# Moving the conversion of one expert's second weight matrix from one product to the next

## The chip, the cores and the metric

The kernel runs on one core of one Trainium2 chip. The metric is the device time of one execution in microseconds (us). The engines are TensorE (PE in the profile; its weight loads are PEld), VectorE (DVE), ScalarE (ACT), GpSimd (POOL) and SyncE (SP), whose queue issues most of the DMAs.

## The reference

A random-feature attention is followed by a gated product and a routed layer of experts, all in float32:

```python
q_p, k_p = phi(q_s), phi(k_s)            # exp(h - max h), h = x omega^T - |x|^2/2
num / den                                # from kv = k_p^T v and z = sum k_p; x is [1152, 512]
h = ((x @ w1) * (x @ w2)) @ w3           # 512 -> 1024 -> 1024
x = h @ w_out                            # [1152, 512]
logits = x @ w_gate                      # 8 experts; argmax picks one for each token
h = np.maximum(disp[e] @ w1[e], 0)       # [capacity, 1024], capacity 288
out[i] = gate_w[i] * (h @ w2[e])[pos[i]] # tokens over the capacity stay zero
```

Here `disp[e]` holds the tokens sent to expert e, in order, as far as the capacity goes.

## The kernel before

Every float32 product is made of three TensorE products: each operand is split into a high part (a cast that ACT makes) and a low part (the difference, a subtraction on DVE or POOL), and high x high, low x high and high x low are summed in PSUM (the list `PASS`). `w3 @ w_out` is multiplied out beforehand into eight tiles `W`, so that the tokens' gated values go straight to 512 features.

The experts run in chunks of 288 token slots, called runs. Two runs are written out, r0 and r1; a loop at the end takes whatever chunks are left over, and has none here. A run consists of these generators, each of which gives way after a piece of its products:

- `to_features` (letter t for r0, T for r1): transposes the gathered rows and splits them into `xc`.
- `product` (p, P): multiplies `W` with `xc` into four PSUM banks `x2p`, one for each 128 of the 512 features, 24 matmuls each. Two steps take the first two slices of all four banks; then a step each finishes bank 0, 1, 2 and 3 with 18 matmuls and splits it: ACT casts it to `x2h` (L843), DVE subtracts to `x2l` (L844).
- `hidden` (h, H): the first weights of the expert, in four quarters q of two 128-wide half steps f. The first quarter's two half steps go side by side over the four feature slices k, in 24 matmuls; each of the other six half steps takes 12. After a half step ACT casts it with the Relu (L865) and DVE makes the low part (L866) into `hh`. The PSUM banks come from the pools `pm` (two banks, even f) and `pa` (four banks, odd f).
- `result_t` (s, S): the second weights of the expert times `hh`. For r1 a first group of 24 matmuls (L899, PSUM `r_yt`) makes 128 of the 512 output features transposed, then 72 matmuls (L913) and six transposes the rest; DVE scales by the gate (`r_yo`, L874), and POOL scatters three groups of 96 rows with an indirect DMA each (L875).

The expert's weights come from HBM by numbers known only at run time, in four quarters for the first matrix (`e1`) and four for the second (`e2`). `e_task` makes a task of each quarter: its load, issued on SP (L743) by `pump` as soon as one of two slots in its ring (`wr` for even quarters, `u` for odd ones) is free, and three stages:

```python
push(key, ring, load, [("A", lambda t: hi(t, 0), False),   # ACT: cast of the first half, 128x512
                       ("AV", both, False),                # DVE: its low part; ACT: second cast
                       ("P", lambda t: lo(t, 1), True)])   # POOL: second low part; frees the slot
```

`tick` advances the tasks by one stage each, at most one for an engine and at most two tasks at a time; so four quarters take nine ticks. A task of an expert's weights is started only when its key is in the set `leave`:

```python
while todo and (todo[0]["key"][0][0] != "e" or todo[0]["key"][:2] in leave) and (...):
    active.append(todo.pop(0))
```

The string `END` writes the order out by hand: a generator's letter is one step of it, a dot is a tick, `x` asks for the e1 quarters of r1 and `y` for its e2 quarters, and the digits 1 to 4 give leave to e1 of r0, e2 of r0, e1 of r1 and e2 of r1. When `S` is first reached, `got2` ticks until all e2 quarters of r1 are done. The instructions of every engine run in the order in which they are written (`in_order`, `keep_order`), so a cast that is written ahead of an eviction on ACT also runs ahead of it.

In the trace the digits of a run and of a matrix are left out of the names: `r_e_20h` is quarter 2, first half, high part, of e1 or of e2 of either run. In the order written here, the e1 quarters of r1 come before its e2 quarters.

Of the kernel before, what the change touches and what calls it, by code (L numbers as in the profile page):

```python
# [54 lines left out]

END = "l<kAkrArfAAArfw>AAAA>AA<At.ttLttMt>1K.p..K.p..Rp..p..p..RpF.2h..h.R.h..Fh..h..h..xh..h..s.TT.3sTT..sTT..s..ssy4P..P..P..P..P..P..P.H.H.H.H.H.HHHSSSS"


@with_exitstack
def attention_moe_kernel(ctx: ExitStack, tc: tile.TileContext, qT, kT, v, om, w1, w2, w3, wo, wg, e1, e2, cap, out):
# [901 lines left out]

    for p in END:
        if p == "A":
# [119 lines left out]
```

## Time and profile before

| | |
|---|---|
| median of three runs | 343.3 us (343.2 to 344.44) |
| profiled execution | 342.88 us, of which the span is 341.1 us |
| PE busy in the span | 326.2 us (96%) |
| DVE, ACT, POOL busy | 214.9, 146.4, 134.6 us (63%, 43%, 39%) |
| mean granted TensorE clock | 0.988 of full speed |

All times in the trace are counted from the start of the span. A row of the timeline gives start, duration, engine, line, operation, output <- inputs and, in brackets, how long the engine was idle before it and what ended that. Matmuls are pipelined, so that one is shown with some 0.29 us while the next starts 0.13 us after it; the starts are what tells the pace.

### The profile page before, as it was taken

Reading aid. Unit: us, or ns where it says so; the run is one execution under the profiler, and the core shown is the slowest. Engines: PE = TensorE matmul, PEld = TensorE weight load, DVE = VectorE, ACT = ScalarE, POOL = GpSimd, SP = SyncE. Lnnn points to the kernel's source line nnn. Section 1 sums busy time; section 2 is a strip of 40 time slices with the busy share of each in tenths; the row PEclk is TensorE's granted clock in tenths of the full one; section 3 lists DMA queues with packets and bytes.
Section 4 is the critical chain, followed back from the end, with each engine's and each line's share of the span. In section 5 each row is a group of like instructions: output and inputs, shape, how many; then the busy total and the mean of one; then the engine's idle time right before and its main releaser. Section 6 shows DMA issues by size and latency. Waiting matters only on the chain. (4 is left out here: it accounts for less than half of the span.)

```text
span 341.1 us, 7107 instructions
## 1 busy us (share of the span) xinstructions
PE 326.2 (96%) x2771; PEld 302.1 (89%) x2771; DVE 214.9 (63%) x426; ACT 146.4 (43%) x347; POOL 134.6 (39%) x118
## 2 busy tenths in 40 slices
PE   8899989999999999999999999999999999979991
PEld 6799879999998899898879988899799998969991
DVE  3979999999987854925695780562787435322110
ACT  4899899733221423424335422222635346232100
POOL 2737920233353224355547572015253612370011
PEclk9999999999999999999999999999999999998997
DMA  7985200243455729982435412966699933230001
GB/s 248 397 311 179 85 12 2 78 160 122 141 174 187 256 39 203 186 160 62 144 113 178 132 53 103 267 50 196 220 219 139 260 126 125 58 136 2 1 25 51
DMA packets 25147, 47.76 MB, mean 140 GB/s; under 512 B 3116, under 2 KB 12460, under 8 KB 25110
## 3 DMA queue, kind: packets, MB, share of 16 engines
q1 hardware_dynamic: 16950, 40.18, 39.1%
q10 hardware_dynamic: 7104, 3.54, 7.1%
q0 software_dynamic: 1056, 3.54, 3.7%
q8 instruction: 24, 0.39, 0.5%
q14 instruction: 13, 0.11, 0.1%
HBM read 38.98 MB, written 8.27 MB: 139 GB/s over the span
## 5 line engine op out<-in xcount | busy, mean ns | idle before, releaser
L433 PE MATMUL ab<-xh,w_hl 128*128 128x288 f32 x512 | 107.8, 299 | 1.0 <-ACT a_sb L437 0.8
L433 PEld LDWEIGHTS ab<-xh,w_hl 128*128 128x128 f32 x512 | 83.5, 188 | 3.6 <-issue 1.9
L433 PE MATMUL ab<-xl,w_hl 128*128 128x288 f32 x256 | 75.6, 295 | 0.0
L433 PEld LDWEIGHTS ab<-xl,w_hl 128*128 128x128 f32 x256 | 48.1, 188 | 0.0
L472 PE MATMUL W<-wo_hl,w_hl 128*128 128x512 f32 x192 | 46.4, 397 | 0.0
L472 PEld LDWEIGHTS W<-wo_hl,w_hl 128*128 128x128 f32 x192 | 35.5, 188 | 8.1 <-issue 0.5
L364 POOL TENSOR_TENSOR w_hl<-w_f,w_hl 128x512 fp32r<-128x512 f32 x22 | 29.7, 1364 | 7.7 <-ACT w_hl L360 6.3
L405 DVE STREAM_TRANSPOSE gs<-g 128x576 f32<-128x576 f32 x16 | 19.6, 1225 | 16.1 <-POOL g L446 16.0
L350 DVE TENSOR_SCALAR w_f<-w_raw 128x512 uint32<-128x512 uint32 x22 | 16.5, 749 | 17.7 <-POOL w_hl L364 16.9
L840 PE MATMUL r_x2p<-r_xc,W 128*128 128x288 f32 x192 | 26.8, 297 | 0.2 <-DVE r_yo L874 0.2
L840 PEld LDWEIGHTS r_x2p<-r_xc,W 128*128 128x128 f32 x192 | 25.8, 188 | 0.5 <-DVE r_yo L874 0.4
L360 ACT CAST w_hl<-w_f 128x512 fp32r<-128x512 f32 x22 | 13.7, 624 | 26.8 <-DVE w_f L355 26.5
L331 POOL TENSOR_TENSOR wo_hl<-wo_f,wo_hl 128x512 fp32r<-128x512 f32 x8 | 11.4, 1429 | 34.2 <-PE xT L276 18.4
L480 POOL TENSOR_TENSOR W<-W_raw,W 128x512 fp32r<-128x512 f32 x8 | 10.9, 1358 | 34.8 <-ACT u_all L503 23.6
L437 ACT COPY a_sb<-ab 128x288 f32<-128x288 f32 x32 | 12.7, 398 | 24.6 <-PE ab L433 24.0
L331 POOL TENSOR_TENSOR w_hl<-w_f,w_hl 128x512 fp32r<-128x512 f32 x10 | 14.0, 1403 | 22.4 <-ACT w_hl L330 22.4
L355 DVE SCALAR_TENSOR_TENSOR w_f<-w_raw,w_f 128x512 uint32<-128x512 uint32 x22 | 20.0, 909 | 0.6
L875 POOL DMA_INDIRECT out<-r_yo,r_odx x6 | 5.6, 932 | 35.6 <-DVE r_yo L874 22.7
L446 POOL TENSOR_TENSOR g<-a_sb,b_sb 128x288 f32<-128x288 f32 x12 | 11.6, 966 | 19.9 <-ACT b_sb L445 19.9
L448 DVE TENSOR_TENSOR g<-a_sb,ab 128x288 f32<-128x288 f32 x20 | 8.9, 446 | 14.1 <-PE ab L433 14.1
L210 PE MATMUL pjk<-om_hl,k_hl 128*128 128x256 f32 x108 | 15.1, 292 | 1.5 <-ACT k_hl L198 1.4
L210 PE MATMUL pjq<-om_hl,q_hl 128*128 128x256 f32 x108 | 16.3, 293 | 0.0
(233 smaller groups left out, 692.4 us busy)
## 6 DMA issues: line engine op xcount, KB each, us to landing
w_raw<-in_w SPq DMA_DIRECT2D x32, 512.0 KB, 3.6
wo_raw<-in_wo SPq DMA_DIRECT2D x8, 512.0 KB, 3.7
gd<-gs ACTq DMA_DIRECT2D x12, 288.0 KB, 6.0
v<-in_v SPq DMA_DIRECT2D x9, 260.0 KB, 5.4
k<-in_kT SPq DMA_DIRECT2D x9, 256.0 KB, 4.7
q<-in_qT SPq DMA_DIRECT2D x9, 256.0 KB, 7.2
out<-zero SPq DMA_DIRECT2D x1, 2304.0 KB, 7.9
r_e_0r<-in_e SPq DMA_DIRECT2D x4, 512.0 KB, 4.9
```

Source lines behind the costliest of these rows:

```text
L210: nc.tensor.matmul(out=ps[:, r * 256:(r + 1) * 256], lhsT=t[:, s, k * 128:(k + 1) * 128], rhs=om_hl[:, w], start=(n == 0), stop=(n == 2))
L331: nc.gpsimd.tensor_tensor(out=hl[1], in0=f.bitcast(F32), in1=hl[0].bitcast(F32), op=ALU.subtract)
L350: V.tensor_scalar(out=f, in0=r[:, :, 1], scalar1=3, scalar2=0x3FFFFFF8, op0=ALU.logical_shift_left, op1=ALU.bitwise_and)
L355: V.scalar_tensor_tensor(out=t["f"], in0=r[:, :, 0], scalar=29, in1=t["f"], op0=ALU.logical_shift_right, op1=ALU.bitwise_or)
L360: A.copy(out=h[:, 0], in_=t["f"].bitcast(F32))
L364: nc.gpsimd.tensor_tensor(out=h[1], in0=t["f"].bitcast(F32), in1=h[0].bitcast(F32), op=ALU.subtract)
L405: V.transpose(out=sts[b][:, :, :, f % GF], in_=g_t[f][:, b * S:(b + 1) * S].rearrange("p (j t) -> p j t", t=32))
L433: nc.tensor.matmul(out=p[:, :C], lhsT=w12[f][w][s][:, k, :], rhs=xhl[c][r][:, k], start=(n == 0), stop=(n == 11))
L437: A.copy(out=abp[f, c], in_=p[:, :C])
L446: nc.gpsimd.tensor_tensor(out=g_t[f][:, c * C:(c + 1) * C], in0=abp.pop((f, c)), in1=b_sb, op=ALU.mult)
L472: nc.tensor.matmul(out=p, lhsT=w3_t[f, k // 4][s][:, k % 4, :], rhs=wo_t[k][r], start=(n == 0), stop=(n == 23))
L840: nc.tensor.matmul(out=p4[d][:, :C], lhsT=w_t[f][:, s, d * 128:(d + 1) * 128], rhs=xc[r][f // 4][:, f % 4], start=(f == 0 and (s, r) == (0 ...
```

## The change

The digit 4 moves from behind `y` to behind the last step of r1's `product`, and each of the first five steps of r1's `hidden` is followed by two ticks in place of one. Nothing is added or taken out; the order of casts and subtractions against the evictions changes.

```diff
-END = "l<kAkrArfAAArfw>AAAA>AA<At.ttLttMt>1K.p..K.p..Rp..p..p..RpF.2h..h.R.h..Fh..h..h..xh..h..s.TT.3sTT..sTT..s..ssy4P..P..P..P..P..P..P.H.H.H.H.H.HHHSSSS"
+END = "l<kAkrArfAAArfw>AAAA>AA<At.ttLttMt>1K.p..K.p..Rp..p..p..RpF.2h..h.R.h..Fh..h..h..xh..h..s.TT.3sTT..sTT..s..ssyP..P..P..P..P..P..P4.H..H..H..H..H..HHHSSSS"
```

## Rows read from the trace of the kernel before

**Rows 1.** Table by stretches: start:end, length, busy time of each engine, PEclk, DMA share, GB/s.

```profile
256.00:270.30 14.30, 14.30 (x121) 14.29 (x120) 10.04 (x36) 7.65 (x17) 5.90 (x6) 1.00 0.88 186
...
300.43:317.82 17.39, 15.30 (x99) 14.31 (x97) 5.63 (x11) 5.75 (x13) 4.80 (x4) 0.90 0.15 57
```

**Rows 2.** Timeline of PE at r1's first expert product and the start of its last.

```profile
300.43 0.30 PE L861 MATMUL r_hp<-r_x2h,r_e_00h 128*128 128x288 f32 x1
...
301.89 0.29 PE L861 MATMUL r_hp<-r_x2h,r_e_00l 128*128 128x288 f32 x1
303.98 0.40 PE L861 MATMUL r_hp<-r_x2h,r_e_00h 128*128 128x288 f32 x1 [1.80 <-ACT r_x2h L843]
...
317.82 0.43 PE L899 MATMUL r_yt<-r_h,r_e_00h 128*128 128x288 f32 x2
```

**Rows 3.** Timeline of ACT over r1's product and first expert product.

```profile
293.42 0.40 ACT L843 CAST r_x2h<-r_x2p 128x288 fp32r<-128x288 f32 x1 [3.54 <-PE r_x2p L840]
...
295.82 0.40 ACT L843 CAST r_x2h<-r_x2p 128x288 fp32r<-128x288 f32 x1 [0.96 <-PE r_x2p L840]
302.50 0.62 ACT L756 CAST r_e_20h<-r_e_2r 128x512 fp32r<-128x512 f32 x1 [6.27 <-SPq L1007]
...
303.54 0.39 ACT L843 CAST r_x2h<-r_x2p 128x288 fp32r<-128x288 f32 x1
...
305.15 0.39 ACT L843 CAST r_x2h<-r_x2p 128x288 fp32r<-128x288 f32 x1
...
318.02 0.41 ACT L865 ACTIVATE r_h<-r_hp 128x288 fp32r<-128x288 f32 x1 [1.19 <-PE r_hp L861]
```

**Rows 4.** Timeline of SP: the load of e2's third quarter.

```profile
298.93 0.33 SPq L743 DMA_DIRECT2D r_e_2r<-in_e  x1
```

**Rows 5.** Timeline of POOL: r0's last scatter, then e1's third quarter.

```profile
296.66 0.92 POOL L875 DMA_INDIRECT out<-r_yo,r_odx  x1 [2.60 <-ACT r_x2h L843]
297.60 1.31 POOL L760 TENSOR_TENSOR r_e_20l<-r_e_2r,r_e_20h 128x512 fp32r<-128x512 f32 x1
```

**Rows 6.** Table by stretches: one stretch inside r1's first expert product.

```profile
306.10:309.20 3.10, 3.10 (x13) 3.10 (x14) 0.92 (x2) 0.82 (x2) 0.62 (x1) 0.51 0.00 0
```

**Rows 7.** Timeline of ACT over the first expert product of r0.

```profile
261.15 0.41 ACT L865 ACTIVATE r_h<-r_hp 128x288 fp32r<-128x288 f32 x1 [0.16 <-PE r_hp L861]
261.46 1.13 ACT L756 CAST r_e_10h<-r_e_1r 128x512 fp32r<-128x512 f32 x2
262.75 0.41 ACT L865 ACTIVATE r_h<-r_hp 128x288 fp32r<-128x288 f32 x1 [0.16 <-PE r_hp L861]
...
265.22 0.41 ACT L865 ACTIVATE r_h<-r_hp 128x288 fp32r<-128x288 f32 x1 [1.04 <-PE r_hp L861]
...
270.02 0.41 ACT L865 ACTIVATE r_h<-r_hp 128x288 fp32r<-128x288 f32 x1 [1.19 <-PE r_hp L861]
```

**Rows 8.** Timeline of PE: the first matmul of r0's first expert product.

```profile
256.17 0.30 PE L861 MATMUL r_hp<-r_x2h,r_e_00h 128*128 128x288 f32 x1
```

**Rows 9.** Timeline of POOL: two low halves of weights.

```profile
251.92 1.86 POOL L760 TENSOR_TENSOR r_e_30l<-r_e_3r,r_e_30h 128x512 fp32r<-128x512 f32 x1 [1.88 <-ACT r_e_30h L756]
...
262.67 1.28 POOL L760 TENSOR_TENSOR r_e_10l<-r_e_1r,r_e_10h 128x512 fp32r<-128x512 f32 x1 [0.30 <-ACT r_e_10h L756]
```

**Rows 10.** Timeline of DVE: two low halves of weights and two small additions.

```profile
247.11 1.79 DVE L760 TENSOR_TENSOR r_e_20l<-r_e_2r,r_e_20h 128x512 fp32r<-128x512 f32 x1
...
260.51 0.69 DVE L760 TENSOR_TENSOR r_e_00l<-r_e_0r,r_e_00h 128x512 fp32r<-128x512 f32 x1
...
263.06 0.90 DVE L944 TENSOR_TENSOR ni<-tm 96x1 int32<-96x1 f32 x1
...
264.03 0.15 DVE L947 TENSOR_TENSOR d<-ends 96x8 f32<-96x8 f32 x1
```

**Rows 11.** Timeline of POOL: r1's first and last scatter.

```profile
326.54 0.92 POOL L875 DMA_INDIRECT out<-r_yo,r_odx  x1 [19.81 <-DVE r_yo L874]
...
335.39 0.92 POOL L875 DMA_INDIRECT out<-r_yo,r_odx  x1 [2.58 <-DVEq L1007]
```

## Prediction, made before the changed kernel was run

> **What bounds the kernel now.** PE is busy for 326.2 of the 341.1 us, so the first view is the table by stretches: where is PE not busy, or not at full clock? For the expert products the two runs can be set side by side. In r0's first expert product PE is busy in all of 14.30 us at a granted clock of 1.00; in r1's it is busy in 15.30 of 17.39 us at 0.90 [rows 1]. Both do the same 96 matmuls. The second view, the timeline of PE, shows where the time goes in r1: twelve matmuls run at 0.13 us each from 300.43 to 301.89, the thirteenth starts at 303.98, and an ACT cast of `x2h` at L843 released it [rows 2]. The third view, the timeline of ACT, tells why that cast was late [rows 3]. Banks 0 and 1 of `x2p` were cast at 293.42 and 295.82, 2.40 us apart, which is the pace of their 18 matmuls; bank 2 was therefore full at 298.22 and bank 3 at 300.62. But bank 2 was cast at 303.54 and bank 3 at 305.15. The ACT row ahead of them is a cast of weights, at 302.50, for which ACT stood idle 6.27 us.
>
> That cast is of the third quarter of e2, and its data came late: SP issued the load at 298.93 [rows 4], because the slot came free only with POOL's low half of e1's third quarter at 297.60, which stood in POOL's queue behind r0's last scatter at 296.66 [rows 5]. So the chain is scatter, POOL subtraction, slot, load (3.57 us from 298.93 to 302.50), ACT cast, and behind that cast, by order alone, two evictions that have nothing to do with it. PE then pays twice: it waits, and in the stretch from 306.10 to 309.20 that follows the wait its granted clock is 0.51, the lower of its two levels, 1.2 GHz [rows 6].
>
> **The change part by part.** No instruction is added. What moves is the conversion of e2's four quarters for r1: eight casts on ACT, four subtractions on DVE, four on POOL.
>
> Which ticks go where: six ticks lie between digit 3 and `y`, and nine are needed for e1's four quarters, so the first three ticks among the P steps still go to e1, before and after. The other ten there belong to e2 before, and do nothing after. The new places hold eleven ticks (one behind digit 4, two behind each of five steps), and e2 needs nine: the last stage falls behind the fourth step, half step f = 4. Nothing is left over for `got2` to force.
>
> The loads don't move: a slot comes free with the POOL stage of e1's quarters, which is one of the same three ticks, so SP still issues e2's third quarter at about 298.93, with nothing queued differently. It lands at 302.5 as before, where no one waits for it until the cast behind half step f = 3, some 6 us later.
>
> What goes: without the weights' casts ahead of them, the casts of banks 2 and 3 start as PE ends them, at about 298.2 and 300.6. The cast takes 0.40 us [rows 3]; if the low part took 0.69 us, the length of a low half of weights nearly twice its size [rows 10], bank 3 would be complete at 301.7. The first expert product reaches slice 2 at 300.43 + 12 x 0.133 = 302.0 and slice 3 at 302.8. So both are there in time, with 1.1 us to spare, and PE should run through. What is late next: e1's third and fourth quarter, whose low halves end on POOL at 298.9 and, one such subtraction later, at 300.2; they are wanted after 48 and 72 matmuls, at 306.8 and 310.0. Nothing there.
>
> The size, by r0's product: from its first matmul at 256.17 [rows 8] to its last Relu cast at 270.02 it takes 13.85 us. One gap between its Relu casts is 2.47 us (262.75 to 265.22) instead of the 1.60 of the others [rows 7], since products of r1's routing lie between; without them it is 13.85 - 0.87 = 12.98 us. Put at r1's first matmul, 300.43, the last Relu cast comes at 313.41 instead of 318.02 [rows 3]: **4.61 us less**. By parts: 303.98 - 302.02 = 1.96 us is the first wait, 3.10 x (1 - 0.51) = 1.52 us the lower clock, and the remaining 1.13 us the second wait, for bank 3, between 303.98 and 306.10.
>
> What it costs: the eight casts now stand between the Relu casts. In r0's product that same pattern is in the trace, and that is why I take this cost as nothing: Relu cast, two weight casts (1.13 us), next Relu cast 1.60 us after the first, and the idle time of 0.16 us before it is ended by PE, so ACT still waits for PE and not PE for ACT [rows 7]. ACT would be full to 1.44 of 1.60 us for four half steps. If that cover went (casts only some 10% longer), evictions would lag, and PE would notice only when a bank is wanted again: f = 4 reuses the bank of f = 0, 3.3 us later. The low halves on DVE (0.69 us) [rows 10] and POOL (1.28 us) [rows 9] go once per half step, 1.97 us if one waits for the other, against a pace of 1.60: at worst they slip by 0.4 us per quarter. The second quarter-stage of e2 can start once f = 0 and f = 1 are done, at 303.6; four times 1.97 us later is 311.5. The first result product starts at 317.82 - 4.6 = 313.2 [rows 2] and wants the last half quarter after 21 matmuls, at 316.0. That is 4.5 us of slack. From below: could the moved work gain something where it was? In the P steps PE had no wait but the one counted; so no gain beyond the 4.61. From above, the slowest rows of such halves are 1.79 us on DVE [rows 10] and 1.86 us on POOL [rows 9]; what they would do is the second rival. I take the nearest rows, those of r0's product, which are the same work at the same place.
>
> One observation weighs against this. In r0's product a DVE addition of 96x1 elements took 0.90 us from 263.06, while one of 96x8 took 0.15 [rows 10]; the long one ended at 263.96, and a POOL subtraction of weights ran from 262.67 to 263.95 [rows 9]. The Trainium skill ("SBUF — State Buffer", section "Who interferes with whom") has a rule for it: a DVE instruction with both inputs in SBUF and a POOL instruction that reads SBUF take the same port, and whoever is second waits for the whole of the first. The trace agrees. By the rule each low half on DVE can wait for the POOL half of the quarter before, and the Relu's low part behind it as well; by the free durations alone it would not. The sum is the same by both, but the rule is a reason to give the second rival a chance at all.
>
> What follows the product moves as a block: the first scatter is released by DVE's scaled rows at 326.54, the last comes 8.85 us later, at 335.39 [rows 11], and all three hang on PE's result products.
>
> **The sum.** The profiled execution is 342.88 us (span 341.1 and 1.8 around it); less 4.6 that is 338.3. The median of the runs, 343.3, is 0.4 above it; less 4.6 that is 338.7. I forecast **338.5 us**, 1.4% faster. What a measurement of this kernel can tell from no change is about 0.5%, so from 341.6 to 345.0 counts as the same.
>
> **The rivals.**
> *The lower clock comes anyway* (in the changed kernel too, TensorE is at 1.2 GHz for some 3 us of this product). For it: that the drop is caused by the wait is read from their order only. Against it: r0's product, without a wait, is at 1.00 throughout [rows 1]. It gives back 1.5 us: 340.0. Chance 0.07.
>
> *The conversions become the chain* (DVE and POOL taking turns, then the casts too). They have from 303.6 to 316.0, which is 3.1 us per quarter. At the slowest rows, 1.79 + 1.86 = 3.65, they end at 318.2, 2.2 late: 340.7. If both casts (1.13) come in series as well, 4.78 per quarter, they end at 322.7, 6.7 late, and the wait in `result_t` brings the lower clock for another 1.5: 346.7, **slower than before**. The point from which it loses is 4.25 us per quarter (4.6 us late). For it: those rows exist. Against it: the halves in r0's product, 0.69 and 1.28, are far from it. Chances 0.06 for the partial loss, 0.04 for slower.
>
> *No change*: the gain is eaten at the end, because the scatters, each waiting for the one before, and not the products set it. For it: the last scatter is not released by its own data. Against it: the first one is, after 19.81 us idle [rows 11], so the series would start earlier. Or the casts stay where they were, if I have miscounted the ticks. 343. Chance 0.06.
>
> **How the numbers follow.** The forecast has 0.77, and its own spread is about 0.9 us either way, from the spread of the runs and from the two ways of counting. The range 337.6 to 340.8 takes in the rival with the clock and the partial loss and leaves out no change and slower. Faster by over 0.5%: 0.77 + 0.07 + 0.06 = 0.90; same 0.06; slower 0.04.
>
> **What would show it.** Right: in the changed profile the `x2h` casts of banks 2 and 3 start at about 298.2 and 300.6; PE has no wait in the first expert product; the granted clock there is 1.00; the first result product starts at about 313.2; the weight casts lie between Relu casts, until about 310; the span is some 336.5 us. Wrong: a PE wait at L861 that is still released by L843 (the order is not the cause), a clock well under 1 without a wait ahead (first rival), a PE wait at L899 or L913 released by ACT, DVE or POOL at L756 or L760 (second), or the first scatter not earlier than 326 (third).

## The result, and the profile after

The changed kernel takes **338.18 us** (median of four runs, 337.45 to 339.21), the kernel before, run beside it, 343.29 us. The ratio is 0.9837, with a 95% interval of 0.9809 to 0.9865. Run once more, beside the last two experiments below, its ratio was 0.9851 (0.9808 to 0.9894). The forecast was 338.5 us.

The table by stretches, as in [rows 1]; the columns are length, busy time and count of PE, PEld, DVE, ACT and POOL, granted clock, DMA share and GB/s. The stretch runs from the first matmul of r1's first expert product to the first result product:

```profile
301.40:314.19 12.79, 12.79 (x98) 12.79 (x97) 6.67 (x12) 7.38 (x16) 6.80 (x4) 1.00 0.19 77
```

12.79 us stand against 17.39, so 4.60 us are gone. PE is busy all the time, and at full clock.

PE's waits from 285 us to the end (who waited for whom, us in total, times, longest) hold nothing at L861 any more, and nothing at L899. First the line of the kernel before that is gone, then all lines of the changed kernel:

```profile
PE r_hp L861 <- ACT r_x2h L843: 2.0, 2, 1.8
```

```profile
PE r_py L905 <- ACT r_y L902: 0.2, 1, 0.2
PE r_x2p L840 <- DVE r_yo L874: 0.2, 1, 0.2
```

The timeline of ACT, against [rows 3]:

```profile
299.20 0.40 ACT L843 CAST r_x2h<-r_x2p 128x288 fp32r<-128x288 f32 x1 [2.00 <-PE r_x2p L840]
301.60 0.40 ACT L843 CAST r_x2h<-r_x2p 128x288 fp32r<-128x288 f32 x1 [2.00 <-PE r_x2p L840]
301.90 0.62 ACT L756 CAST r_e_00h<-r_e_0r 128x512 fp32r<-128x512 f32 x1
304.39 0.82 ACT L865 ACTIVATE r_h<-r_hp 128x288 fp32r<-128x288 f32 x2 [1.87 <-PE r_hp L861]
...
306.39 0.41 ACT L865 ACTIVATE r_h<-r_hp 128x288 fp32r<-128x288 f32 x1 [0.16 <-PE r_hp L861]
306.70 0.61 ACT L756 CAST r_e_10h<-r_e_1r 128x512 fp32r<-128x512 f32 x1
307.21 0.62 ACT L756 CAST r_e_20h<-r_e_2r 128x512 fp32r<-128x512 f32 x1
307.99 0.41 ACT L865 ACTIVATE r_h<-r_hp 128x288 fp32r<-128x288 f32 x1 [0.16 <-PE r_hp L861]
308.30 0.61 ACT L756 CAST r_e_21h<-r_e_2r 128x512 fp32r<-128x512 f32 x1
308.81 0.62 ACT L756 CAST r_e_30h<-r_e_3r 128x512 fp32r<-128x512 f32 x1
309.59 0.41 ACT L865 ACTIVATE r_h<-r_hp 128x288 fp32r<-128x288 f32 x1 [0.16 <-PE r_hp L861]
309.90 0.61 ACT L756 CAST r_e_31h<-r_e_3r 128x512 fp32r<-128x512 f32 x1
...
314.39 0.41 ACT L865 ACTIVATE r_h<-r_hp 128x288 fp32r<-128x288 f32 x1 [1.19 <-PE r_hp L861]
```

Banks 2 and 3 are cast the moment PE has filled them: the bracket says that ACT waited for PE, where before the cast at 302.50 waited for a load. The weight casts stand in pairs between the Relu casts, and the 0.16 us ended by PE says that they fit, as in r0's product [rows 7].

The load itself is as late as it was. SP, against [rows 4]:

```profile
299.84 0.33 SPq L743 DMA_DIRECT2D r_e_2r<-in_e  x1
```

The low halves of e2 on POOL and the last one on DVE:

```profile
305.79 1.68 POOL L760 TENSOR_TENSOR r_e_00l<-r_e_0r,r_e_00h 128x512 fp32r<-128x512 f32 x1 [4.74 <-ACT r_e_00h L756]
307.44 1.73 POOL L760 TENSOR_TENSOR r_e_10l<-r_e_1r,r_e_10h 128x512 fp32r<-128x512 f32 x1
309.14 1.74 POOL L760 TENSOR_TENSOR r_e_21l<-r_e_2r,r_e_21h 128x512 fp32r<-128x512 f32 x1
310.85 1.74 POOL L760 TENSOR_TENSOR r_e_31l<-r_e_3r,r_e_31h 128x512 fp32r<-128x512 f32 x1
```

```profile
310.41 1.03 DVE L760 TENSOR_TENSOR r_e_30l<-r_e_3r,r_e_30h 128x512 fp32r<-128x512 f32 x1
```

They are stretched (1.74 us instead of 1.28, 1.03 instead of 0.69) but end at 312.59. The last of them is the operand of the twenty-fourth result product, at 314.19 + 23 x 0.133 = 317.25: 4.7 us of slack.

The first and the last scatter, against [rows 11]:

```profile
322.91 0.92 POOL L875 DMA_INDIRECT out<-r_yo,r_odx  x1 [10.32 <-DVE r_yo L874]
...
331.49 0.92 POOL L875 DMA_INDIRECT out<-r_yo,r_odx  x1 [3.27 <-DVEq L1007]
```

The two profiled spans differ by 3.8 us (341.1 and 337.3), not 4.6, and the parts say why. The profiled execution after came 0.97 us later to r1's first expert product (301.40 against 300.43). That lies ahead of everything that was changed: PE's first long wait, near 10 us, is 2.0 us in the trace after and 1.4 in the trace before, and the rest builds up over the next 250 us. Then 4.60 us less in the product, 0.27 less from the first result product to the last scatter (17.30 against 17.57), 0.10 more behind it (5.81 against 5.71): -3.80. Over the runs, the medians differ by 5.1 us.

### The profile page after: what moved, and what is told of

It is laid out like the page before. It is cut to its first block, busy times and chain, and to the rows that moved or that the text cites. A ratio compares the mean times of both kernels' runs of the same rounds, so it can differ in the third digit from the quotient of the medians.

```text
span 337.3 us, 7102 instructions
## 1 busy us (share of the span) xinstructions
PE 323.7 (96%) x2771; PEld 300.5 (89%) x2771; DVE 216.2 (64%) x426; ACT 146.5 (43%) x347; POOL 135.8 (40%) x118
## 5 line engine op out<-in xcount | busy, mean ns | idle before, releaser
L331 POOL TENSOR_TENSOR wo_hl<-wo_f,wo_hl 128x512 fp32r<-128x512 f32 x8 | 10.9, 1359 | 35.0 <-PE xT L276 18.4
L480 POOL TENSOR_TENSOR W<-W_raw,W 128x512 fp32r<-128x512 f32 x8 | 10.9, 1357 | 35.0 <-ACT u_all L503 23.6
L760 POOL TENSOR_TENSOR r_e_00l<-r_e_0r,r_e_00h 128x512 fp32r<-128x512 f32 x4 | 6.0, 1511 | 28.7 <-ACT r_e_00h L756 20.8
L210 PEld LDWEIGHTS pjk<-om_hl,k_hl 128*128 128x128 f32 x108 | 13.7, 193 | 3.1 <-issue 2.2
```

The costliest lines, as they stand in the source:

```text
L210: nc.tensor.matmul(out=ps[:, r * 256:(r + 1) * 256], lhsT=t[:, s, k * 128:(k + 1) * 128], rhs=om_hl[:, w], start=(n == 0), stop=(n == 2))
L331: nc.gpsimd.tensor_tensor(out=hl[1], in0=f.bitcast(F32), in1=hl[0].bitcast(F32), op=ALU.subtract)
```

## The experiments

All are written as another order string; each ratio is to the kernel before on the same chip, whose median was 344.52 us in the first group (e1 to e4) and 343.66 in the second. The parts of the string shown begin where r1's e1 gets leave.

**The digit alone** (e1): without the second ticks.

```diff
-3sTT..sTT..s..ssy4P..P..P..P..P..P..P.H.H.H.H.H.HHHSSSS
+3sTT..sTT..s..ssyP..P..P..P..P..P..P4.H.H.H.H.H.HHHSSSS
```

> Only the digit 4 moves behind r1's product; the five steps of hidden keep one tick each, so the last casts of e2's fourth quarter are written behind the last Relu cast. Theory (the order on ACT ahead of banks 2 and 3 of x2p is the cause): the wait in the first expert product is gone, PE runs through it at a clock of 1.00. By the changed kernel's trace the first result product starts at 314.2 and wants the last low half at 317.0; here its two casts come after the last Relu cast, at about 314.7 to 315.8, and POOL's 1.3 us end at about 317.1. So at most 0.5 us of wait: 338.2 to 338.8 us. Rival (the two ticks make the gain, since conversions that lag hold up the result products): 340 us or more, with PE waits at L899 or L913.

Measured: 338.59 us, ratio 0.9834 (0.9798 to 0.9870). The gain is all there without the ticks. The timelines of ACT, POOL and PE show how close it is:

```profile
313.49 0.41 ACT L865 ACTIVATE r_h<-r_hp 128x288 fp32r<-128x288 f32 x1 [1.19 <-PE r_hp L861]
313.80 0.61 ACT L756 CAST r_e_30h<-r_e_3r 128x512 fp32r<-128x512 f32 x1
314.31 0.62 ACT L756 CAST r_e_31h<-r_e_3r 128x512 fp32r<-128x512 f32 x1
```

```profile
315.06 1.28 POOL L760 TENSOR_TENSOR r_e_31l<-r_e_3r,r_e_31h 128x512 fp32r<-128x512 f32 x1 [2.11 <-ACT r_e_31h L756]
```

```profile
316.09 0.43 PE L899 MATMUL r_yt<-r_h,r_e_31h 128*128 128x288 f32 x2
316.39 0.40 PE L899 MATMUL r_yt<-r_h,r_e_31l 128*128 128x288 f32 x1
```

POOL's last half ends at 316.34 and the product that reads it starts at 316.39, some 0.03 us later than the pace would have it, and the next matmul starts 0.24 us behind it, at 316.63, instead of 0.13. So the conversion is only just in time: the second ticks buy over 4 us of slack, and no more than 0.15 us of time.

**Only the last two quarters move** (e2): leave stays where it was; the ticks between the last P steps are taken out, and the first two steps of `hidden` are followed by two ticks each, in place of one behind each of five.

```diff
-3sTT..sTT..s..ssy4P..P..P..P..P..P..P.H.H.H.H.H.HHHSSSS
+3sTT..sTT..s..ssy4P..P..P..PPPP.H..H..HHHHHHSSSS
```

> As the kernel before, but without ticks between the last steps of r1's product, so that only e2's third and fourth quarter move into hidden; the first and second stay among the P steps. Theory (only the casts that wait for the late loads harm): as the changed kernel, 338.2 us, banks 2 and 3 cast within 0.1 us of PE's last matmul of each. Rival (any weight cast among the P steps costs, as ACT time ahead of the evictions): between the two kernels, 339.5 to 342 us.

Measured: 338.31 us, ratio 0.9821 (0.9788 to 0.9855). ACT:

```profile
294.07 1.14 ACT L756 CAST r_e_10h<-r_e_1r 128x512 fp32r<-128x512 f32 x2
296.17 0.40 ACT L843 CAST r_x2h<-r_x2p 128x288 fp32r<-128x288 f32 x1 [0.96 <-PE r_x2p L840]
298.57 0.40 ACT L843 CAST r_x2h<-r_x2p 128x288 fp32r<-128x288 f32 x1 [2.00 <-PE r_x2p L840]
300.97 0.40 ACT L843 CAST r_x2h<-r_x2p 128x288 fp32r<-128x288 f32 x1 [2.00 <-PE r_x2p L840]
302.94 0.62 ACT L756 CAST r_e_20h<-r_e_2r 128x512 fp32r<-128x512 f32 x1 [1.56 <-SPq L1007]
```

The second quarter's casts stand ahead of bank 1 as before and cost nothing, because their data were there; ACT still waits for PE, 0.96 us. Even here the third quarter's cast waits for its load (1.56 us), but what stands behind it is a Relu cast that PE has not finished yet. So neither the leave nor the place among the P steps is what cost time; the two quarters with late data were.

**The loads come earlier** (e3): the casts stay among the P steps, ahead of the evictions; three ticks more ahead of r0's scatters let POOL make e1's low halves first.

```diff
-3sTT..sTT..s..ssy4P..P..P..P..P..P..P.H.H.H.H.H.HHHSSSS
+3sTT...sTT...s...ssy4P..P..P..P..P..P..P.H.H.H.H.H.HHHSSSS
```

> The kernel before with its digit 4 in its old place, so all e2 casts stay ahead of the evictions of banks 2 and 3; but one tick more in each of three places ahead of r0's last step, so that POOL makes e1's third and fourth quarters before r0's three scatters and SP can issue the loads of e2 some 9 us earlier. Theory (root cause is the slot behind the scatters): loads issued by about 290, no idle ACT ahead of a cast of e2, banks 2 and 3 at most 1.1 us late, which the order of the first quarter covers: 338.2 to 338.7 us. Rival (the casts' place among the P steps is what costs, whenever their data come): about 343 us. Third possibility: the three ticks disturb r0's last products: over 339 us with waits between 272 and 289 us.

Measured: 338.84 us, ratio 0.9842 (0.9809 to 0.9876). SP, then ACT:

```profile
288.06 0.33 SPq L743 DMA_DIRECT2D r_e_2r<-in_e  x1
289.00 0.33 SPq L743 DMA_DIRECT2D r_e_3r<-in_e  x1
```

```profile
290.36 1.14 ACT L756 CAST r_e_10h<-r_e_1r 128x512 fp32r<-128x512 f32 x2 [1.29 <-DMA r_e_1r<-in_e]
...
294.29 0.62 ACT L756 CAST r_e_20h<-r_e_2r 128x512 fp32r<-128x512 f32 x1
...
296.39 0.40 ACT L843 CAST r_x2h<-r_x2p 128x288 fp32r<-128x288 f32 x1 [0.96 <-PE r_x2p L840]
296.69 0.62 ACT L756 CAST r_e_30h<-r_e_3r 128x512 fp32r<-128x512 f32 x1
297.21 0.62 ACT L756 CAST r_e_31h<-r_e_3r 128x512 fp32r<-128x512 f32 x1
298.79 0.40 ACT L843 CAST r_x2h<-r_x2p 128x288 fp32r<-128x288 f32 x1 [0.96 <-PE r_x2p L840]
301.19 0.40 ACT L843 CAST r_x2h<-r_x2p 128x288 fp32r<-128x288 f32 x1 [2.00 <-PE r_x2p L840]
```

The load is issued 10.9 us earlier than in [rows 4], and with it the casts among the P steps are as good as in the new place. Their place is not quite the old one: with three ticks more ahead of them, the third quarter's casts stand between the evictions of banks 0 and 1 and the fourth's between 1 and 2, each one eviction earlier than before. That alone could not have helped, since a cast that waits for a late load would hold up one eviction more from there. So this shows the root of the wait: the slot that came free only behind r0's scatters. The time is just above the 338.2 to 338.7 us expected, beside a kernel before that took 344.52 in this group. One thing was expected otherwise: ACT does wait once, 1.29 us, for the load of the second quarter; no eviction was due then, and it cost nothing. Of the third possibility there is a trace: PE's wait at the start of r1's product is 0.5 us instead of 0.2, since DVE scales r0's rows behind one more low half.

**Only the last quarter moves** (e4): the ticks behind the fifth and the sixth P are taken out; `hidden` has two ticks behind its first step and none behind the others.

```diff
-3sTT..sTT..s..ssy4P..P..P..P..P..P..P.H.H.H.H.H.HHHSSSS
+3sTT..sTT..s..ssy4P..P..P..P..PPP.H..HHHHHHHSSSS
```

> As the kernel before, but only e2's fourth quarter moves into hidden; the late third one is still cast ahead of bank 2. Theory: PE still waits for bank 2 until about 304.0 (1.96 us), but bank 3 follows at once, so the second wait (1.1 us) goes: 342.2 us if the drop of the clock (1.5 us) belongs to the first wait alone, 340.7 us if the clock stays at 1.00 because the pause is shorter. Rival (the two waits are one and the same delay): 343.3 us, unchanged.

Measured: 342.74 us, ratio 0.9938 (0.9912 to 0.9964). PE's timeline, and the table by stretches over the product and over the slow part of it:

```profile
303.94 0.40 PE L861 MATMUL r_hp<-r_x2h,r_e_00h 128*128 128x288 f32 x1 [1.86 <-ACT r_x2h L843]
304.43 0.40 PE L861 MATMUL r_hp<-r_x2l,r_e_00h 128*128 128x288 f32 x1
```

```profile
300.32:317.11 16.79, 14.84 (x98) 14.39 (x97) 5.32 (x11) 5.74 (x13) 5.05 (x4) 0.90 0.15 61
305.60:308.90 3.30, 3.30 (x16) 3.30 (x15) 1.51 (x3) 1.33 (x3) 1.21 (x1) 0.50 0.00 0
```

The first wait is there alone, and the clock falls behind it as it did before. The wait for bank 3 went, but the product is shorter by 0.60 us only (16.79 against 17.39), not by 1.13. The two rows of PE show a part that stays: the matmul with the low part of bank 2 starts 0.49 us after the one with its high part instead of 0.13, so 0.36 us belong to DVE's half of bank 2's eviction and not to bank 3. And the slow stretch is 3.30 us here, against 3.10 in [rows 6]. By their mean granted clock, both outcomes that the theory named came up, though only the first of the eight executions, one with the drop, was traced. Six had a mean granted clock of 0.988 or 0.989 and took 342.2 to 343.2 us; one had 0.994 and took 341.39, one 0.997 and took 340.64.

**All conversion just ahead of the result products** (e5): the second rival's chain by itself.

```diff
-3sTT..sTT..s..ssy4P..P..P..P..P..P..P.H.H.H.H.H.HHHSSSS
+3sTT..sTT..s..ssyP..P..P..P..P..P..PHHHHHHHH4SSSS
```

> The digit 4 stands behind the last step of hidden, with no ticks in it, so that all of e2's conversion is forced just ahead of the result products. This measures the second rival's chain by itself. In the times of the changed kernel's trace the casts start at 314.7, behind the last Relu cast; eight of them 0.52 us apart take ACT to 318.9, and POOL's four low halves follow each other from 315.8, at 1.3 us each to 321.0, or at 1.74 us each, as they took beside DVE's in the changed kernel, to 322.8. The first group of 24 result products wants the last of them at 317.25. Theory (POOL's chain of low halves sets it): late by 3.6 to 5.5 us, PE waits at L899 released by POOL at L760, and a lower clock behind it of up to 1.6 us: 341.8 to 345 us. Rival (the result products take what is there and the conversion keeps up): below 341 us.

Measured: 343.96 us, ratio 1.0021 (0.9998 to 1.0044): the whole gain is lost, and not more. Of PE's six waits at L899 four were released by POOL at L760, one by DVE there and the first by ACT's cast. POOL, DVE and PE:

```profile
314.84 1.27 POOL L760 TENSOR_TENSOR r_e_00l<-r_e_0r,r_e_00h 128x512 fp32r<-128x512 f32 x1 [15.07 <-ACT r_e_00h L756]
316.08 1.74 POOL L760 TENSOR_TENSOR r_e_10l<-r_e_1r,r_e_10h 128x512 fp32r<-128x512 f32 x1
317.77 1.72 POOL L760 TENSOR_TENSOR r_e_21l<-r_e_2r,r_e_21h 128x512 fp32r<-128x512 f32 x1
319.45 1.73 POOL L760 TENSOR_TENSOR r_e_31l<-r_e_3r,r_e_31h 128x512 fp32r<-128x512 f32 x1
```

```profile
316.59 1.77 DVE L760 TENSOR_TENSOR r_e_20l<-r_e_2r,r_e_20h 128x512 fp32r<-128x512 f32 x1
318.29 1.76 DVE L760 TENSOR_TENSOR r_e_30l<-r_e_3r,r_e_30h 128x512 fp32r<-128x512 f32 x1
```

```profile
314.30 0.53 PE L899 MATMUL r_yt<-r_h,r_e_00h 128*128 128x288 f32 x2 [1.01 <-ACT r_e_00h L756]
...
321.24 0.40 PE L899 MATMUL r_yt<-r_h,r_e_31l 128*128 128x288 f32 x1 [0.47 <-POOL r_e_31l L760]
```

From the second quarter on POOL and DVE go in step, 1.68 to 1.70 us per quarter from one start to the next, while each row shows 1.7 us or more on both engines. The rows overlap: a row's duration holds the time in which the other engine has its turn. The first matmul behind this group starts at 321.47; from this execution's start of `hidden`, 300.35, the changed kernel's 12.79 us and 24 matmuls would have led to 316.3. So the chain is some 5.1 us late, inside the 3.6 to 5.5 expected, and without a lower clock in this execution.

**The conversion from the fourth step on** (e6): some 3.7 us later than in the changed kernel (POOL's first low half starts at 308.70, and this execution runs 0.8 us ahead of the other).

```diff
-3sTT..sTT..s..ssy4P..P..P..P..P..P..P.H.H.H.H.H.HHHSSSS
+3sTT..sTT..s..ssyP..P..P..P..P..P..PHHH4..H..H..H..H..HSSSS
```

> The digit 4 stands behind the fourth half step of hidden, with two ticks behind each step from there: the conversion starts some 4.4 us later than in the changed kernel. Theory (there are 4 us of slack): POOL's last low half ends at about 316.3 in the times of the changed kernel's trace, wanted at 317.25: no wait, 338.2 us, same as the changed kernel. Rival (the conversion is as tight as DVE and POOL waiting for each other can make it): PE waits at L899, 339.5 us or more.

Measured: 338.12 us, ratio 0.9825 (0.9787 to 0.9864), beside 0.9851 for the changed kernel in the same group. No PE wait; POOL's last half ends at 315.11 and is wanted at 316.45:

```profile
313.55 1.56 POOL L760 TENSOR_TENSOR r_e_31l<-r_e_3r,r_e_31h 128x512 fp32r<-128x512 f32 x1
```

```profile
316.45 0.29 PE L899 MATMUL r_yt<-r_h,r_e_31l 128*128 128x288 f32 x1
```

So the slack is real, and the place of the conversion inside `hidden` is free within some 4 us. Of the changed kernel, run again with this group:

> The changed kernel once more, to stand on the same chip beside the two that follow: the same ratio to the kernel before as in the first comparison, 0.981 to 0.987.

Measured: 338.57 us, as expected. No order tried here beats it by more than the intervals leave open, and with PE at no wait in r1's expert product there is nothing left in it for this edit to take.

## Why the prediction was right

*What bounds it.* The chain scatter, POOL half, slot, load, cast, eviction was right at each link that was tested: with an earlier slot (e3) casts among the P steps cost nothing; with the old slot, moving the two late quarters alone (e2) brings the gain; with one of them left in place (e4) the first wait remains at 1.9 us.

*The ticks.* The count was right: e1's three ticks stay among the P steps, e2's nine fall behind the half steps, the last behind f = 4 (the cast at 309.90 follows the Relu cast at 309.59), and nothing is left for `got2`. One place was miscounted: the first cast that needs the late load was put behind f = 3, some 6 us after the load landed, and came behind f = 2, at 307.21, some 4 us after it. It waited for nothing, so this cost nothing.

*The size.* 4.61 us were forecast from r0's product, 4.60 came in the trace. This total was read off a product that ran without a wait and not added up from the parts, so it did not need them to be right. Banks 2 and 3 were to be cast at 298.2 and 300.6, the first result product to start at 313.2; less the 0.97 us by which this execution was late from the start, they came at 298.23, 300.63 and 313.22.

*The parts of it* were less well told apart. The 1.13 us put down to bank 3 were mis-sized: e4, which takes that wait away, gains 0.60 in the trace, and 0.36 belong to the low part of bank 2, which starts 0.49 us behind the high part in the kernel before as well. And the clock is not a fixed term. Of the 13 executions of the kernel before in the second group, two had a mean granted clock of 0.997 and took 341.93 and 342.25 us; the eight at 0.989 or less took 343.5 to 344.9. The mean is over the whole span, and in the trace before it also holds a clock of 0.62 from 335.00 to 341.10, where PE has no matmul left. A mean of 0.997 leaves 0.003 x 340 = 1.0 us of lost clock for everything, less than the 1.52 of the product's drop alone, so the two executions can't have had that drop in full. By this estimate it is worth about 2 us where it comes, and the gain is about 3.5 us without it (338.57 against 341.9 to 342.3) and 5 or more with it; no trace of the kernel before without the drop was taken. The 1.52 us read from the one profile were a sample of this; 4.6 us would give a ratio of 0.9866, and the measured one is 0.9837 with 0.9865 as its upper end, so over the runs the gain was somewhat larger than that execution's.

*The cover.* The cost of the moved casts was nothing, as r0's product had shown. POOL's and DVE's halves did get in each other's way, as the small addition in [rows 10] had hinted: the rows on POOL are 1.68 to 1.74 us long and start 1.65 to 1.71 us apart. That is less than the 1.97 allowed for, and close to the half step's 1.60, so they slipped by 0.1 us a quarter.

*The second rival* was priced wrongly, and this did not matter only because it didn't come. It added the slowest row of DVE, 1.79, to the slowest of POOL, 1.86, and the casts to both. e5 puts the chain itself on the path: 1.68 to 1.70 us per quarter in all, with rows of 1.77 and 1.74 in it. Rows like those hold waiting already, and adding them counts the same time twice. At 1.70 the chain is far from the 4.25 us per quarter at which the change would have lost. The Trainium skill ("SBUF — State Buffer", section "Who interferes with whom") says that DVE with two inputs in SBUF and a POOL instruction that reads SBUF hold the port in turns, each for its whole instruction. The trace agrees as to the turns, and less as to the whole: in e5, from the end of one engine's row to the end of the other's, it is 0.54 and 0.56 us for DVE (318.36 behind 317.82, 320.05 behind 319.49) and 1.13 for POOL, each some 0.15 less than the undisturbed 0.69 and 1.28, so that much of each row runs beside the other's.

*No change* fell with the first scatter: it came at 322.91, released by DVE's rows, 3.6 us earlier than [rows 11].

Left open: why the clock falls in some executions and not in others. In e5's profiled execution PE waited six times at L899, 3.1 us in all and at most 1.0 at once, with the granted clock at 1.00 from 312 to 328; in e4's one wait of 1.9 us was followed by a stretch at 0.50. Two executions are too few for a rule, and no run here separated the length of a wait from its place.

## What to carry to other kernels

When an engine's queue holds an instruction that waits for a transfer, look at what is written behind it: here two evictions of 0.4 us waited for a load that they did not use. Either move the waiting instruction behind them, or look further back for what makes the load late; in one group of runs the first was worth 5.9 us (e1) and the second 5.7 (e3). Before adding up rows of two engines that may be taking turns, read the start-to-start time of a series of them, since a row can hold the other's time.

## What the runs showed of the hardware that was not expected

In one group of 13 executions the kernel before ran at a mean granted clock of 0.983 to 0.989 in eight and at 0.992 to 0.997 in five, and took up to 3 us less in these (341.93 against 344.89 us); in the other group all 11 stood at 0.984 to 0.988. DVE and POOL subtractions of 128x512 that meet settle into a step of some 1.70 us on both engines in e5, with 1.72 to 1.77 us shown for each row, where alone they show 0.69 and 1.28.
